# Fused attention and two feed-forward layers: scores of the next chunk placed inside the bundles of value products

## The chip, the cores and the metric

One core of a Trainium2 chip runs the whole program in one launch. The metric is device time in microseconds (us). Engines are named as in the profile: PE is TensorE (matrix products; PEld is its load of the stationary operand), DVE is VectorE, ACT is ScalarE, POOL is GpSimd, SP is SyncE, which issues all DMAs.

## What is computed

Attention for 2 batches of 8 heads, 576 positions and 64 numbers per head, with a learned bias that depends on the distance of two positions, then two feed-forward layers over the 1152 x 512 result. Cut to what matters here:

```python
def _attn_ref(q, k, v, w1, b1, w2):
    scores = scale * np.matmul(q, k.transpose(0, 1, 3, 2))
    ...
    bias = h @ w2
    scores = scores + bias.transpose(2, 0, 1)[None, :, :, :]
    scores = scores - np.max(scores, axis=-1, keepdims=True)
    attn = np.exp(scores)
    attn = attn / (np.sum(attn, axis=-1, keepdims=True) + 1e-09)
    return np.matmul(attn, v).astype(np.float32)
```

## The kernel before

The program has three stages: the bias is made (to about 64 us of the profile), attention runs (about 72 to 197 us), the two feed-forward layers follow (197 to the end).

Attention goes through eight **units**, a unit being two heads of one batch. A unit has two **jobs**, `sub` 0 with 4 chunks of 128 query rows and `sub` 1 with 5, so a unit takes nine **slots**, one chunk `n` each (`run_slot`, L464). The chunk with `n` = 2 of `sub` 1 is mixed: its rows come from both heads, and its scores take 8 products where the others take 4. Of a chunk the kernel makes:

- its **scores** (`scores`, L287): products of 288 columns into a PSUM tile `ps`, of which there are two (L154); a stationary operand of 128 x 128. PE waits here until the chunk two before has left its `ps`, and in the first chunks of a job for `ql`, the low part of q, which POOL makes (L191).
- bias and row minimum on DVE (L324, out of `ps`), the exponential on ACT (L338), sums and reciprocals on DVE (L342, L343), the scaling on POOL (L346).
- three slots (LAG) after a job's last chunk its probabilities begin to be **transposed** on PE (L373) in **pieces**, one or two pieces a slot: `PIECES` has five pieces for `sub` 0 (0, 1, 2, 3, last) and six for `sub` 1 (0, 1, 2, 3, f, last). In the next slot ACT or DVE copies the transposed piece from PSUM to `at` (L380).
- the **value products** of a whole job (`values`, L383) are done together when its last piece is there: a **bundle**. Their stationary operand is 128 x 64, so a product fills one half of the array's columns and of PSUM's partitions, the first head in one half and the second in the other. In `sub` 0 each piece has one product of 256 columns for either half. In `sub` 1 a piece has 320 columns for the first half, and 128 + 64 for the second; piece f has four products of 128 columns, all for the second half; piece last has 64 + 256 columns for either half.
- in the slot after a bundle the results are **finished** (L408): ACT copies `po` out of PSUM (L423 or L429), DVE and POOL make the splits and differences that the next layer needs.

Every engine works through its instructions in the written order (`tc.manual_schedule`, L524). Within a slot PE's order is the scores of this chunk, the transposes, and, where a job's last piece is there, the bundle. So the bundle of `sub` 0 stands between the scores of chunks 2 and 3 of the next unit's `sub` 0 (in the first unit that has one, between chunks 1 and 2), and that of `sub` 1 between chunks 3 and 4 of the next unit's `sub` 1. There are 14 such bundles while chunks are left, two in each unit but the first; the last unit's two bundles come after all chunks, in the tail (185 to 197 us).

Of the kernel before, what the change touches and what calls it, by code (L numbers as in the profile page):

```python
# [26 lines left out]
AHEAD = 2  # L27

LAG = 3

BATCHES = ((0,), (1, 2), (3,)), ((0, 1), (2, 3), (4,))

# [66 lines left out]
def tile_kernel(ctx: ExitStack, tc, qT, kT, vS, wb, wg, wv, wo, wi, wo2, table, out):  # L99
# [25 lines left out]
    with ExitStack() as actx:  # L125
# [36 lines left out]
        def load_k(i):  # L162

            pr, b = UNITS[i]
            kr = bias[0][:, :2] if i > 2 else rawp.tile([P, 2, S], F32, tag="kr", name="kr")
            load(kr, kT, pr, b)
            return dict(i=i, pr=pr, b=b, kr=kr)
# [25 lines left out]
        def prepare_k(u):  # L193


            kst = u["kst"] = kp.tile([P, 2, S], F32R, tag="kst", name="kst")
            kr = u["kr"]
            for a in range(2):
                high(kst[:, a], kr[:, a], KHIGH[a])
                yield  # L200
                for hf in range(2):
                    rows, cols = slice(D - D * hf, P - D * hf), slice(HALF * hf, HALF * (hf + 1))
                    low(kst[rows, a, cols], kst[rows, a, cols], kr[rows, a, cols], KLOW[2 * a + hf])
                yield

        def prepare_q(u, sub):


            qr = u["qr"]
            width = 704 if sub else 512  # L210
            qh = qp.tile([P, width], F32R, tag=f"qh{sub}", name="qh")
            ql = qp.tile([P, width], F32R, tag=f"ql{sub}", name="ql")
            sm = smp.tile([P, 4, 5], F32, name="sm")
            if sub == 0:
                parts = [(0, 0, 0, 256), (1, 256, 0, 256)]
                chunks = [(0, 0), (1, 0), (0, 1), (1, 1)]
            else:
                parts = [(0, 0, 256, 320), (1, 384, 256, 320)]
                nc.gpsimd.memset(qh[:, 320:384].bitcast(F32), 0.0)
                nc.gpsimd.memset(ql[:, 320:384].bitcast(F32), 0.0)  # L220
                chunks = [(0, 0), (1, 0), ("mix",), (0, 1), (1, 1)]
            u[sub] = dict(u, sub=sub, qh=qh, ql=ql, chunks=chunks, sm=sm, es=[], last=[], at={})
            for j, (a, o, s0, w) in enumerate(parts):
                high(qh[:, o : o + w], qr[:, a, s0 : s0 + w], QHIGH[2 * sub + j])
                yield
                low(ql[:, o : o + w], qh[:, o : o + w], qr[:, a, s0 : s0 + w], QLOW[2 * sub + j])
                yield
# [59 lines left out]
        def scores(u, n):  # L287

            sub, pr, kst = u["sub"], u["pr"], u["kst"]
            ch = u["chunks"][n]  # L290
            ps = psS.tile([P, 2, 512], F32, tag="S", name="ps")
            if ch[0] == "mix":
                heads = [(0, 256), (1, 320)]
                bt = bias[4][:, pr]
            else:
                a, c = ch
                heads = [(a, (448 if sub else 256) * a + P * c)]
                bt = bias[2 * sub + c][:, 2 * pr + a]

            parts = [(t, a, o) for t in ("ql", "qh") for a, o in heads]  # L300
            for hf in range(2):
                for i, (t, a, o) in enumerate(parts):
                    nc.tensor.matmul(  # L303
                        ps[:, hf, :HALF],
                        u[t][:, o : o + P],
                        kst[:, a, HALF * hf : HALF * (hf + 1)],
                        start=i == 0,
                        stop=i == len(parts) - 1,
                    )
            return ps, bt  # L310
# [72 lines left out]
        def values(u, piece):  # L383

            if piece == 0:
                u["po"] = psO.tile([P, 512], F32, name="po")
            at = u["at"].pop(piece)
            if piece == "f":
                parts = [(jc, 1, 1, 128, P * jc, 128) for jc in range(4)]
            elif piece == "last":  # L390
                mixed = [(4, 0, 0, 256, 256, D), (4, 1, 2, 256, 320, D)] if u["sub"] else []
                parts = mixed + [(4, a, a, 0, 0, 256) for a in range(2)]
            elif u["sub"]:
                parts = [(piece, 0, 0, 0, 0, 320), (piece, 1, 1, 0, 384, 128), (piece, 1, 2, 256, 320, D)]
            else:
                parts = [(piece, a, a, 0, 256 * a, 256) for a in range(2)]

            for jc, a, t, o, i, n in parts:
                v = u["v"][:, jc] if jc < 4 else u["vt"]
                nc.tensor.matmul(  # L400
                    u["po"][D * a : D * (a + 1), o : o + n],
                    v[:, D * t : D * (t + 1)],
                    at[:, i : i + n],
                    start=piece == 0 and o == 0,
                    stop=jc == 4 and o == 0,
                )
# [51 lines left out]
        chunks = [(i, sub, n) for i in range(2 * NP) for sub in range(2) for n in range(4 + sub)]  # L458
        jobs, turned, gathered, done, spare = [], [], [], [], itertools.cycle([False, True])
        prep = itertools.chain(prepare_k(units[0]), prepare_q(units[0], 0))  # L460
        before = None
        slot = 0

        def run_slot():  # L464
            nonlocal turned, done, prep, before, slot
            if slot < len(chunks):
                i, sub, n = chunks[slot]
                if n == 0:
                    for _ in prep:
                        pass  # L470
                    if sub == 0:
                        if i + 1 < 2 * NP:
                            units.append(load_k(i + 1))
                        if i == NP:
                            flat = lambda ap: ap.rearrange("p a s -> p (a s)")
                            pairs[2:] = [flat(bias[c][:, 2 * a : 2 * a + 2]) for a in range(2) for c in (2, 3)]
                            mixes[1] = flat(bias[4][:, :2])[:, : 5 * P]
                            nc.gpsimd.memset(mixes[1][:, S:], 0.0)
                        prep = prepare_q(units[i], 1)
                    elif i + 1 < 2 * NP:  # L480
                        load_qv(units[i + 1])
                        prep = itertools.chain(prepare_k(units[i + 1]), prepare_q(units[i + 1], 0))
                u = units[i][sub]
                got = scores(u, n)
            for w in done:
                w["eager"] = slot >= len(chunks) - 1
                late.append(finish(w))
                if w["eager"]:
                    next(late[-1])
            done = []  # L490
            for w, piece, got_t in turned:
                gather(w, piece, *got_t)
            if slot < len(chunks):
                biased(u, n, *got)
            if before:
                softmax(*before)
                before = None
            for _ in range(2):
                next(prep, None)
            late[:] = [steps for steps in late if next(steps, late) is not late]  # L500
            held, turned = [t[:2] for t in turned], []

            over = slot >= len(chunks)
            for _ in range(2 if slot % 9 in TWICE or over else 1):
                if jobs and jobs[0][2] <= slot:
                    w, piece, _ = jobs.pop(0)
                    turned.append([w, piece, transposes(w, piece, over and (piece == "f" or next(spare)))])
            gathered.extend(held)

            ends = [i + 1 for i, (w, piece) in enumerate(gathered) if piece == PIECES[w["sub"]][-1]]  # L510
            last_job = over and gathered and gathered[0][0] is units[-1][1]
            for _ in range(len(gathered) if last_job else max(ends, default=0)):
                w, piece = gathered.pop(0)
                values(w, piece)
                if piece == PIECES[w["sub"]][-1]:
                    done.append(w)
            if slot < len(chunks):
                before = (u, n)
                if n == 3 + sub:
                    jobs.extend((u, piece, slot + LAG) for piece in PIECES[sub])  # L520
            slot += 1
# [483 lines left out]
    with tc.manual_schedule(engines={E.PE}):  # L1005
        quads = {"z": z}
        for q in range(4):
# [5 lines left out]
            for word in f"{OTHER if q else FIRST} {TAIL}".split():  # L1013
                who, what = word
                if who in "tu":
                    n = int(what)
# [60 lines left out]
```

## Time and profile before

| | |
|---|---|
| three runs | 600.58, 601.92, 603.95 us; median 601.92 |
| profiled execution | 600.55 us, span of its instructions 598.5 us |
| PE | busy 582.8 us (97%) |
| DVE, ACT, POOL | busy 460.3, 376.2, 111.5 us |
| TensorE clock granted | 0.999 of full speed |

In the rows below a time at the start of a row is in us from the span's start. PE's products are pipelined: the durations of single rows overlap, so the text takes the distance between the starts of two rows. A product of `values` stands as two MATMUL records, one of `scores` or a transpose as one. `128*64` or `128*128` is the stationary operand. In square brackets stands the engine's idle time before a row, and who ended it.

### The profile page before, as it was taken

The numbers are of one execution on the slowest core, as the hardware profiler recorded it, in microseconds if no ns is written. First come the engines' busy times: TensorE is split into PE (matmuls) and PEld (weight loads), VectorE is DVE, ScalarE is ACT, GpSimd is POOL, SyncE is SP. The second block draws the span as 40 slices with busy tenths as digits, with TensorE's granted clock in tenths as the row PEclk, the third lists the DMA queues.
The fourth block names the chain that finished last, engine by engine and source line by source line (L and its number), as shares of the span: only waits on it lengthen the run. The fifth ranks groups of instructions, "written<-read, shape, count | busy, mean of one in ns | idle before, by whom it ended". The sixth has DMA issues, their size and how long they took to land.

```text
span 598.5 us, 11379 instructions
## 1 busy us (share of the span) xinstructions
PE 582.8 (97%) x4274; PEld 516.7 (86%) x4274; DVE 460.3 (77%) x982; ACT 376.2 (63%) x715; POOL 111.5 (19%) x165
## 2 busy tenths in 40 slices
PE   8899799999999999999999999999999999999997
PEld 6343588888887999999999999999989989988986
DVE  7999578878888999897689735679998976983432
ACT  5998787879888876665558424349835734732520
POOL 0301587878993000000000000000000000000000
PEclk9999999999999999999999999999999999999999
DMA  8979923334432333324225222122444240400012
GB/s 221 207 197 208 214 63 99 91 110 111 110 119 89 117 98 108 103 75 137 73 79 190 84 71 71 71 75 70 138 130 134 90 141 5 137 36 1 2 51 106
DMA packets 47414, 63.30 MB, mean 106 GB/s; under 512 B 4480, under 2 KB 35200, under 8 KB 47360
## 3 DMA queue, kind: packets, MB, share of 16 engines
q1 hardware_dynamic: 47360, 62.59, 36.7%
q8 instruction: 33, 0.54, 0.4%
q14 instruction: 21, 0.17, 0.1%
HBM read 49.60 MB, written 2.36 MB: 87 GB/s over the span
## 4 chain that ended last, share of the span: by engine, by line
PE 81%; DVE 7%; ACT 4%; DMA 4%; issue 2%; POOL 2%; SPq 0%; DVEq 0%; ACTq 0%; POOLq 0%
PE pw L684 37%; PE pw L992 16%; PE pw L635 13%; PE ps L303 5%; PE po L400 5%; PE pt L373 4%; DVE r L258 3%; DMA bias<-st 2%; ACT st L278 1%; DMA e<-in_qT_dram 1%; ACT r L256 1%; POOL ql L191 1%; PE pb L266 1%; ACT e L338 1%; DMA G<-in_table_dram 1%
## 5 line engine op out<-in xcount | busy, mean ns | idle before, releaser
L992 PE MATMUL pw<-oh,g2h 128*128 128x512 f32 x144 | 56.2, 390 | 0.0
L992 PE MATMUL pw<-oh,g2l 128*128 128x512 f32 x144 | 56.1, 390 | 0.0
L992 PE MATMUL pw<-ol,g2h 128*128 128x512 f32 x144 | 56.1, 389 | 0.0
L303 PE MATMUL ps<-kst,ql 128*128 128x288 f32 x160 | 49.3, 337 | 4.5 <-POOL ql L191 3.4
L266 PE MATMUL pb<-r,wb_sb 128*32 128x288 f32 x576 | 49.1, 412 | 4.4 <-ACT st L278 2.7
L258 DVE TENSOR_SCALAR r<-G 128x576 f32<-128x576 f32 x108 | 51.5, 553 | 0.1
L635 PE MATMUL pw<-gh,sh 128*128 128x384 f32 x144 | 48.4, 336 | 0.0
L635 PE MATMUL pw<-gh,sl 128*128 128x384 f32 x144 | 48.4, 336 | 0.0
L635 PE MATMUL pw<-gl,sh 128*128 128x384 f32 x144 | 48.3, 336 | 0.0
L266 PEld LDWEIGHTS pb<-r,wb_sb 128*32 128x32 f32 x576 | 20.3, 109 | 31.5 <-ACT st L278 11.5
L609 DVE SCALAR_TENSOR_TENSOR x<-raw,x 128x512 int32<-128x512 int32 x68 | 46.2, 686 | 0.9
L303 PEld LDWEIGHTS ps<-kst,ql 128*128 128x128 f32 x160 | 29.0, 188 | 16.3 <-DVE sm L324 5.7
L303 PE MATMUL ps<-kst,qh 128*128 128x288 f32 x160 | 42.6, 294 | 0.0
L324 DVE CUSTOM_DVE_ANT_0 e<-ps,bias 128x576 f32<-128x576 f32 x44 | 33.0, 749 | 9.0 <-PE ps L303 7.6
L346 POOL TENSOR_SCALAR e<-e,sm 128x576 f32<-128x576 f32 x44 | 34.1, 784 | 25.2 <-DVE sm L343 19.4
L380 ACT COPY at<-pt 128x512 f32<-128x512 f32 (+2 forms) x69 | 36.2, 547 | 3.6 <-PE pt L373 3.4
L338 ACT ACTIVATE e<-e,sm 128x576 f32<-128x576 f32 x44 | 34.3, 780 | 6.1 <-DMA vt<-in_vS_dram 3.4
L400 PE MATMUL po<-at,v 128*64 128x256 f32 (+3 forms) x384 | 36.8, 332 | 1.0 <-DVE at L380 0.8
L1030 DVE TENSOR_TENSOR acc<-pw,acc 128x512 f32<-128x512 f32 x27 | 17.5, 684 | 25.1 <-PE pw L992 25.1
L606 DVE TENSOR_SCALAR x<-x 128x512 int32<-128x512 int32 x68 | 28.7, 426 | 9.2 <-ACT x L605 5.0
L400 PEld LDWEIGHTS po<-at,v 128*64 128x64 f32 x384 | 26.6, 137 | 8.0 <-issue 1.7
L992 PEld LDWEIGHTS pw<-oh,g2l 128*128 128x128 f32 x144 | 27.0, 188 | 5.8
(272 smaller groups left out, 1678.2 us busy)
## 6 DMA issues: line engine op xcount, KB each, us to landing
raw<-in_wo_dram SPq DMA_DIRECT2D x28, 512.0 KB, 3.6
bias<-st SPq DMA_DIRECT2D x32, 288.0 KB, 4.7
raw<-in_wi_dram SPq DMA_DIRECT2D x16, 512.0 KB, 3.8
raw<-in_wv_dram SPq DMA_DIRECT2D x12, 512.0 KB, 4.2
raw<-in_wg_dram SPq DMA_DIRECT2D x12, 512.0 KB, 3.5
qr<-in_qT_dram SPq DMA_DIRECT2D x14, 288.0 KB, 4.1
v<-in_vS_dram SPq DMA_DIRECT2D x8, 384.0 KB, 3.4
bias<-in_kT_dram SPq DMA_DIRECT2D x10, 288.0 KB, 4.2
```

The lines of the kernel that those rows point to most:

```text
L258: nc.vector.tensor_scalar(r, G[:, w0 : w0 + S], PB[:, n : n + 1], 0.0, op0=ALU.add, op1=ALU.max)
L266: nc.tensor.matmul(pb[32 * ct : 32 * ct + 32, hf, :HALF], W2, rs[ct][:, HALF * hf : HALF * (hf + 1)], start=True, stop=True,)
L303: nc.tensor.matmul(ps[:, hf, :HALF], u[t][:, o : o + P], kst[:, a, HALF * hf : HALF * (hf + 1)], start=i == 0, stop=i == len(parts) - 1,)
L324: nc.vector.tensor_tensor_reduce(out=e[:, :S].rearrange("p (a n) -> p a n", a=2), in0=ps[:, :, :HALF], in1=bt.rearrange("p (a n) -> p a n" ...
L338: nc.scalar.activation(e, e, AF.Exp, bias=sm[:, 0, n : n + 1], scale=-1.0, accum_out=sm[:, 1, n : n + 1])
L346: nc.gpsimd.tensor_scalar(e, e, sm[:, 3, i : i + 1], 1.0, op0=ALU.mult, op1=ALU.mult)
L380: marks[eng, u["i"], u["sub"]] = copy(at[:, :w], pt[:, :w]).ins
L400: nc.tensor.matmul(u["po"][D * a : D * (a + 1), o : o + n], v[:, D * t : D * (t + 1)], at[:, i : i + n], start=piece == 0 and o == 0, stop ...
L609: nc.vector.scalar_tensor_tensor(yi, lw, 29, yi, op0=ALU.logical_shift_right, op1=ALU.bitwise_or)
L635: nc.tensor.matmul(ps[:, :n], w[:, k], x, start=first and k == 0 and i == 0, stop=last and k == NK - 1 and i == 2)
L684: nc.tensor.matmul(ps[:, hf, :HALF], a[:, o + k], b[:, HALF * hf : HALF * (hf + 1)], start=start and k == 0 and i == 0, stop=k == 1 and i ...
L992: nc.tensor.matmul(ps, g, w.rearrange("p k f -> p (k f)"), start=f == 0 and i == 0, stop=f == 3 and i == 2)
```

## The change

Where a bundle has given its third product group (index 2, `MIDDLE`) and the job at hand has a chunk left, the scores of that next chunk are issued at once, ahead of the fourth piece. The next slot takes them as they are and does not issue them again.

```diff
+MIDDLE = 2
...
         before = None
+        ahead = []
         slot = 0
...
                 u = units[i][sub]
-                got = scores(u, n)
+                got = ahead.pop() if ahead else scores(u, n)
...
-            for _ in range(len(gathered) if last_job else max(ends, default=0)):
+            for j in range(len(gathered) if last_job else max(ends, default=0)):
                 w, piece = gathered.pop(0)
                 values(w, piece)
+                if j == MIDDLE and slot < len(chunks) and n < 3 + sub and not ahead:
+                    ahead.append(scores(u, n + 1))
```

The order of the instructions on DVE, ACT, POOL and SP stays as it was; on PE the 14 bundles change, and nothing else. PE at a bundle of `sub` 0, third full unit, before (`po` is the value product's result, `ps` the scores, `pt` a transpose; line numbers of the kernel before):

```order
L373 MATMUL pt<-ident,m_965 128x128
L373 MATMUL pt<-ident,e_960 128x128
L400 MATMUL po<-at,v 64x256 x8
L400 MATMUL po<-at,vt_103 64x256 x2
L303 MATMUL ps<-kst,ql 128x288
L303 MATMUL ps<-kst,qh 128x288
L303 MATMUL ps<-kst,ql 128x288
L303 MATMUL ps<-kst,qh 128x288
L373 MATMUL pt<-ident,e_960 128x128
```

and the same place after the change, where two more lines at the head of the file move all line numbers on by two:

```order
L375 MATMUL pt<-ident,m_965 128x128
L375 MATMUL pt<-ident,e_960 128x128
L402 MATMUL po<-at,v 64x256 x6
L305 MATMUL ps<-kst,ql 128x288
L305 MATMUL ps<-kst,qh 128x288
L305 MATMUL ps<-kst,ql 128x288
L305 MATMUL ps<-kst,qh 128x288
L402 MATMUL po<-at,v 64x256 x2
L402 MATMUL po<-at,vt_103 64x256 x2
L375 MATMUL pt<-ident,e_960 128x128
```

The four products of scores have moved ahead of the last four value products; transposes now follow value products directly. PE at the end of a bundle of `sub` 1 in the same unit, before:

```order
L400 MATMUL po<-at,v 64x320
L400 MATMUL po<-at,v 64x128
L400 MATMUL po<-at,v 64x64
L400 MATMUL po<-at,v 64x128 x4
L400 MATMUL po<-at,vt_103 64x64 x2
L400 MATMUL po<-at,vt_103 64x256 x2
L303 MATMUL ps<-kst,ql 128x288
L303 MATMUL ps<-kst,qh 128x288
L303 MATMUL ps<-kst,ql 128x288
L303 MATMUL ps<-kst,qh 128x288
L373 MATMUL pt<-ident,e_113 128x128
```

and after:

```order
L305 MATMUL ps<-kst,ql 128x288
L305 MATMUL ps<-kst,qh 128x288
L305 MATMUL ps<-kst,ql 128x288
L305 MATMUL ps<-kst,qh 128x288
L402 MATMUL po<-at,v 64x320
L402 MATMUL po<-at,v 64x128
L402 MATMUL po<-at,v 64x64
L402 MATMUL po<-at,v 64x128 x4
L402 MATMUL po<-at,vt_103 64x64 x2
L402 MATMUL po<-at,vt_103 64x256 x2
L375 MATMUL pt<-ident,e_113 128x128
```

Here the scores have moved ahead of pieces 3, f and last: 11 of the bundle's 20 value products now come behind them.

## Rows read from the trace of the kernel before

**Rows 1.** The chain that ended last: a sub 1 bundle, and its longest piece.
```profile
116.33 3.03 PE po L400 x30
...
199.04 127.77 PE pw L684 x960
```
**Rows 2.** Windows between sub 0 bundles: length, PE busy (matmuls), PEclk, DMA share, GB/s.
```profile
74.56:91.29 16.73, 16.73 (x150) 1.00 0.32 82
91.29:107.89 16.60, 16.27 (x142) 1.00 0.42 108
107.89:123.58 15.69, 15.69 (x142) 1.00 0.35 96
123.58:140.18 16.60, 16.26 (x142) 1.00 0.37 98
140.18:156.62 16.44, 16.28 (x142) 1.00 0.41 111
156.62:173.29 16.67, 16.58 (x143) 1.00 0.26 67
```
**Rows 3.** PE's timeline at the first bundle, which follows scores without transposes between.
```profile
73.83 0.40 PE L303 MATMUL ps<-kst,ql 128*128 128x288 f32 x1
...
74.56 1.95 PE L400 MATMUL po<-at,v 128*64 128x256 f32 x16
...
76.87 0.40 PE L303 MATMUL ps<-kst,ql 128*128 128x288 f32 x1
```
**Rows 4.** PE's timeline behind another sub 0 bundle: its last products, scores, transposes.
```profile
109.67 0.60 PE L400 MATMUL po<-at,vt 128*64 128x256 f32 x4
110.20 0.40 PE L303 MATMUL ps<-kst,ql 128*128 128x288 f32 x1
...
110.84 0.38 PE L373 MATMUL pt<-ident,e 128*128 128x128 f32 x2
```
**Rows 5.** PE's timeline in the tail: the last unit's two bundles, in parts.
```profile
189.34 0.65 PE L400 MATMUL po<-at,v 128*64 128x256 f32 x4 [0.77 <-DVE at L380]
...
190.35 0.44 PE L373 MATMUL pt<-ident,e 128*128 128x128 f32 x2
190.63 0.27 PE L373 MATMUL pt<-ident,bias 128*128 128x128 f32 x1
...
192.59 1.26 PE L400 MATMUL po<-at,v 128*64 128x320 f32 x12 [0.27 <-DVE B21l L418]
193.79 0.66 PE L373 MATMUL ps<-ident,e 128*128 128x128 f32 x4
...
194.70 1.44 PE L400 MATMUL po<-at,v 128*64 128x320 f32 x17
...
196.94 0.40 PE L684 MATMUL pw<-B11h,wh 128*128 128x288 f32 x1
```
**Rows 6.** PE's timeline before a mixed chunk's scores, in two units.
```profile
113.21 0.60 PE L373 MATMUL pt<-ident,e 128*128 128x128 f32 x4
113.56 0.51 PE L303 MATMUL ps<-kst,ql 128*128 128x288 f32 x2
...
128.89 0.60 PE L373 MATMUL pt<-ident,e 128*128 128x128 f32 x4
129.69 0.54 PE L303 MATMUL ps<-kst,ql 128*128 128x288 f32 x2 [0.20 <-DVE sm L324]
```
**Rows 7.** Who waited for whom: us in total, times, longest us.
```profile
DVE e L324 <- PE ps L303: 7.6, 9, 1.4
...
DVE bias L324 <- PE ps L303: 5.1, 6, 1.1
```
**Rows 8.** Timelines of PE and DVE: a sub 1 bundle, and the mixed chunk's biased scores.
```profile
132.24 2.41 PE L400 MATMUL po<-at,v 128*64 128x320 f32 x30
...
133.65 0.74 DVE L324 CUSTOM_DVE_ANT_0 m<-ps,bias 128x576 f32<-128x576 f32 x1
```
**Rows 9.** ACT's timeline before the tail.
```profile
184.91 0.43 ACT L423 CAST B21h<-po 128x320 fp32r<-128x320 f32 x1 [1.10 <-PE po L400]
```

## What the change was expected to do

> **What bounds the kernel now.** I read the chain that ended last first. Behind attention it is PE without a break: from 199 us on one piece of 128 us after the other [rows 1]. So whatever attention wins or loses up to PE's first feed-forward product at 196.94 [rows 5] reaches the end undiminished, and the question is when PE gets there.
>
> Inside attention I cut PE's time at the starts of the `sub` 0 bundles [rows 2]. Six stretches, each a whole unit's work on PE, at the full clock in all of them. The third is 15.69 us long and PE is busy throughout: call it quiet. The second, fourth, fifth and sixth hold the same 142 or 143 matmuls and take 16.60, 16.60, 16.44 and 16.67, on average 16.58: there PE waits some 0.89 a unit. The first is 16.73, but with eight more matmuls; four transposes and the step to the next scores take 0.35 [rows 6], so eight are some 0.7 and it is nearly quiet, at 16.0. Where PE waits is seen in [rows 6]: from four transposes to the mixed chunk's scores take 0.35 in the quiet unit and 0.80 in the next one, because DVE has not yet emptied a `ps`.
>
> DVE in its turn waits for scores 15 times, 12.7 us in all [rows 7], about twice a unit, where a bundle stands in front of them. That is what the change attacks. But DVE's waiting is not PE's: in the quiet unit DVE waits as well and PE loses nothing. The whole prize is PE's waits, 4 x 0.89 and a few tenths elsewhere, about 4 us.
>
> **What the change costs on PE.** No instruction is added or removed; PE only changes more often between two kinds of work, and the bundles fall in two.
>
> A `sub` 0 bundle now: 2.31 from its start to the next scores [rows 3], and 0.64 from there to the transposes [rows 4], 2.95 together. After the change there are three steps. Second part, pieces 3 and last followed by transposes: the tail runs exactly this by itself, 189.34 to 190.35, 1.01 [rows 5]. The whole bundle has six passes more than that (each product runs twice, the halves side by side), so a pass is (2.31 - 1.01) / 6 = 0.217, and the first part, two passes more than the second, 1.44. Between them stand the scores: from scores to value products 0.73 at the one place that has this order [rows 3]. And transposes start slower behind value products, 0.28 for two [rows 5]: I add 0.06. Sum 1.44 + 0.73 + 1.01 + 0.06 = 3.24, so **+0.29**.
>
> A `sub` 1 bundle now: 3.03 [rows 1] and 0.64, together 3.67. Here the cut hurts more. A piece has 320 columns for the first half of the array and 192 for the second; pieces f and last make up for it, 832 columns against 320, so that over the bundle both halves have 1600. The second half can run ahead only while nothing else stands between. The tail shows a cut: there the same 20 products run as two pieces, 192.59 to 193.79, and the other 14 products, 194.70 to 196.94 [rows 5]: 1.20 + 2.24 = 3.44 against 3.03. The change cuts one piece later. First part: 1.20 and two passes of 320 columns, 2 x 0.217 x 320/256 = 0.54, so 1.74. Second part: its longer half has 1024 columns where the tail's 14 products have 1216, so an estimate of 2.24 x 1024/1216 = 1.89. Sum 1.74 + 0.73 + 1.89 + 0.06 = 4.42, so **+0.75**.
>
> Seven bundles of each kind: 7 x 1.04 = 7.3 us more on PE.
>
> **What it gives back.** Scores come 2.31 - 1.44 = 0.87 earlier at a `sub` 0 bundle and 3.03 - 1.74 = 1.29 at a `sub` 1 bundle, so DVE's 0.85 on average per wait goes nearly everywhere, and what it does next is ready sooner; and PE, coming later to its own waits by 0.29 or 0.75, finds them shorter for that alone. But a unit cannot be quicker than PE's own work, 15.69 + 1.04 = 16.73.
>
> By stretches: the third is quiet and pays nearly all, 0.95 (a tenth for small waits inside it); the first 0.85, with two tenths of waits to lose; so 1.8. The four long ones go from 16.58 to at least 16.73. I take 0.2 each, because one new wait appears: the scores inside a `sub` 1 bundle need the mixed chunk's `ps`. In the fourth stretch DVE works on that from 133.65 to 134.39, and the bundle starts at 132.24 [rows 8], so the third piece would be through at 132.24 + 1.74 = 133.98, and the scores stand 0.4 unless DVE is early by then. It should be by about that much, since the wait of 0.45 before the mixed chunk in that stretch is the one the `sub` 0 bundle causes. That makes 0.8, between 0 and 4 x 1.04 = 4.2.
>
> The last stretch, 173.29 to 196.94, has its own price. Before the tail ACT stands 1.10 for the result of the last bundle that is cut, with everything else of the tail queued behind [rows 9]: its exponentials, DVE's sums and copies behind them, one of which PE waits 0.77 for [rows 5]. This bundle's result comes 1.74 + 0.73 + 1.89 - 3.03 = 1.33 later, and all of that goes through; earlier scores there help nobody, since ACT's order puts the copy first. With +0.29 for the `sub` 0 bundle and 0.2 off for a wait of the usual kind: +1.4, between 0.7 (only PE's own cost less its waits) and 1.6.
>
> Together 1.8 + 0.8 + 1.4 = **+4.0 us**. The profiled execution took 600.55, so 604.55 by its rows; the median of the three runs, 601.92, is 1.37 above it, and I give the time for the median: **605.9**. The bounds: 1.6 + 0 + 0.7 = +2.3 where every wait gives way, 7.3 + 0.6 (the 1.33 in place of 0.75 at the end) = +7.9 where none does.
>
> **Rivals.**
> 1. *The waits stay.* If the long stretches are held by ACT's and POOL's queues rather than by late scores, PE's extra work adds to them: +5.5 to +7.9, some 608.5. For it: the bundle's result, which ACT and DVE finish, comes 0.87 or 1.33 later. Against: the waits lie on PE's own path, so coming later shortens them.
> 2. *The cut of `sub` 1 costs no more than that of `sub` 0.* The second part was scaled, not seen. At 0.29 for each of 14 a unit needs 15.69 + 0.58 = 16.27: the long ones gain 0.3 each, the quiet two pay 1.0 together, the end 0.5: +0.3, 602.2. Against it stands the tail's 3.44 for 3.03.
> 3. *Faster: the change of kinds is free*, weight loads being hidden. Then only waits change: the four long stretches fall to 15.69, -3.6 us, 598.3. It decides where a unit's added PE work stays under its 0.89 of waits. Against it: scores behind value products start 0.53 after the last four products' row begins, 0.31 of it after the last pass [rows 4], where a pass takes 0.217. The Trainium skill has this rival's rule on its page "TensorE: Matmul & The Clock Gate", section "Step-by-step: what each phase is for": weight loads are pulled ahead of products in flight. Its page "TensorEngine Tiling (Array Packing)", section "Key Properties", says the contrary for this case: a change of tiling mode drains the engine; by that rule, the trace agrees.
>
> That nothing moves is excluded by the order: all 14 places change.
>
> **How the numbers follow.** Forecast 0.6 (+2.3 to +5.5), first rival 0.15, second 0.19, third 0.06. About 0.5%, 3.0 us, is what a measurement here can tell from no change: the forecast lies under it in 0.07 of its 0.6. So slower 0.68, same 0.26, faster 0.06. The range goes from the second rival to the lower part of the first: 602.0 to 608.5.
>
> **What would show it.** In the profile after: `sub` 0 bundles with their scores and up to the transposes 3.2 long, `sub` 1 bundles 4.4; DVE's waits for scores well under 12.7 us; all six stretches at 16.7 to 17.0, the quiet one gone; ACT's wait before the tail 2.4 in place of 1.10. The forecast is wrong if second parts of `sub` 1 take 1.5, if the third stretch stays near 15.7, or if the long ones pass 17.3.

## The result and the profile after

| | before | after |
|---|---|---|
| median | 601.72 us (6 runs, 600.58 to 604.23) | 608.37 us (6 runs, 607.59 to 609.69) |
| profiled execution | 600.55 us, span 598.5 | 607.6 us, span 605.8 |
| PE's first feed-forward product | 196.94 [rows 5] | 204.20 |

The change makes the kernel slower by 1.1%: ratio 1.0112, 95% interval 1.0093 to 1.013, or 6.65 us between the medians. 605.9 was forecast, by a sum of +4.0. The time lies in the range, at its upper end.

In the changed kernel most line numbers are two higher than before: scores are L305, transposes L375, value products L402, DVE's biased scores L326. The chain that ended last (start, us, engine, tile, line) is shown around the sub 1 bundle of the fourth stretch, and where the feed-forward begins:

```profile
134.73 0.57 ACT kst L187
135.32 0.98 DVE kst L193
136.34 0.91 DVE T1l L420
137.24 0.60 DVE at L382
137.84 0.67 DVE m L326
138.57 0.79 PE ps L305 x4
139.36 1.91 PE po L402 x17
...
206.31 127.79 PE pw L689 x960
```

The last row answers to the second of [rows 1]: still one piece of 128 us, 7.3 later. What is new stands above it. The chain leaves PE in the middle of a bundle and goes through DVE: PE stands until DVE has read the mixed chunk's scores (tile `m`). Before, it ran through the same work of ACT and DVE in this stretch (131.13 to 133.72), but came back to PE only later, through POOL's `ql`.

The windows that answer to [rows 2], each from one sub 0 bundle's start to the next, the last one from there to the first feed-forward product (length, PE busy, PEclk, DMA share, GB/s):

```profile
74.72:93.30 18.58, 18.58 (x151) 0.94 0.25 62
93.30:110.81 17.51, 16.66 (x142) 1.00 0.36 93
110.81:127.40 16.59, 16.59 (x142) 1.00 0.38 101
127.40:144.93 17.53, 16.68 (x142) 1.00 0.34 93
144.93:162.35 17.42, 16.65 (x142) 1.00 0.35 96
162.35:179.30 16.95, 16.95 (x142) 1.00 0.32 83
179.30:204.20 24.90, 23.74 (x210) 1.00 0.34 107
```

| stretch | 1 | 2 | 3 | 4 | 5 | 6 | last |
|---|---|---|---|---|---|---|---|
| forecast change | +0.85 | +0.2 | +0.95 | +0.2 | +0.2 | +0.2 | +1.4 |
| measured change | +1.85 | +0.91 | +0.90 | +0.93 | +0.98 | +0.28 | +1.25 |

The third, the sixth and the last came as forecast. The second, fourth and fifth lost 0.9 to 1.0 each where 0.2 was expected. PE's busy time in them is 0.77 to 0.85 short of the length, so PE waits there, as it did before the change. The first stretch has a loss of its own: PEclk is 0.94.

What PE does at the two kinds of bundle, where nothing is waited for (third stretch, PE's timeline; brackets hold idle time and its releaser):

```profile
110.81 1.52 PE L402 MATMUL po<-at,v 128*64 128x256 f32 x12
112.26 0.40 PE L305 MATMUL ps<-kst,ql 128*128 128x288 f32 x1
...
112.99 0.65 PE L402 MATMUL po<-at,v 128*64 128x256 f32 x4
...
114.01 0.44 PE L375 MATMUL pt<-ident,e 128*128 128x128 f32 x2
...
119.30 1.83 PE L402 MATMUL po<-at,v 128*64 128x320 f32 x18
121.06 0.40 PE L305 MATMUL ps<-kst,ql 128*128 128x288 f32 x1
...
121.79 1.10 PE L402 MATMUL po<-at,v 128*64 128x320 f32 x11
...
123.70 0.55 PE L375 MATMUL pt<-ident,e 128*128 128x128 f32 x3
```

The sub 0 bundle is 1.45 + 0.73 + 1.02 = 3.20 long, against 2.95 before. The sub 1 bundle is 1.76 + 0.73 + 1.91 = 4.40, against 3.67. These are the forecast's 3.18 and 4.36 without its 0.06 for the transposes. In the fourth stretch the same bundle looks otherwise on PE:

```profile
135.89 1.83 PE L402 MATMUL po<-at,v 128*64 128x320 f32 x18
138.57 0.40 PE L305 MATMUL ps<-kst,ql 128*128 128x288 f32 x1 [0.85 <-DVE sm L326]
```

DVE's timeline beside it:

```profile
135.32 0.98 DVE L193 TENSOR_TENSOR kst<-bias,kst 64x288 fp32r<-64x288 f32 x1 [1.03 <-ACT kst L187]
...
137.77 0.74 DVE L326 CUSTOM_DVE_ANT_0 m<-ps,bias 128x576 f32<-128x576 f32 x1
```

From first product to scores take 2.68 in place of 1.76: PE stands 0.92, and in the second and fifth stretch 0.92 and 0.84. DVE reaches the mixed chunk 137.77 - 127.40 = 10.37 after the stretch's start. Before it was 133.65 - 123.58 = 10.07 [rows 2, 8]. So it comes 0.3 later, not earlier.

Its work did not begin late. In each unit four subtractions make the low part of `kst`, the next unit's k: three on POOL and one on DVE, which stands ahead of T1l (a low part that the next layer needs), a copy and the mixed chunk. These are DVE's and POOL's second one before the change, and POOL's second one after it:

```profile
131.73 0.46 DVE L191 TENSOR_TENSOR kst<-bias,kst 64x288 fp32r<-64x288 f32 x1 [0.79 <-ACT kst L185]
...
131.84 1.00 POOL L191 TENSOR_TENSOR kst<-bias,kst 64x288 fp32r<-64x288 f32 x1
...
135.19 0.79 POOL L193 TENSOR_TENSOR kst<-bias,kst 64x288 fp32r<-64x288 f32 x1
```

DVE's subtraction for `kst` starts 135.32 - 127.40 = 7.92 after the stretch's start, where it was 131.73 - 123.58 = 8.15: 0.23 earlier. But it takes 0.98 in place of 0.46. Before, it started ahead of POOL's second subtraction for `kst`, and POOL's took 1.00. Now POOL's three have moved forward further, from 7.38 to 6.92 after the stretch's start, so that POOL's second one starts first and takes 0.79, and DVE's is the long one. In the second stretch the same happens (0.99 in place of 0.46). In the fifth it starts 0.30 later and takes 1.59 in place of 0.46:

```profile
152.85 1.59 DVE L193 TENSOR_TENSOR kst<-bias,kst 64x288 fp32r<-64x288 f32 x1 [0.86 <-ACT kst L187]
```

In the third stretch, where DVE starts first (118.43, POOL's at 118.45), it takes 0.46 and PE does not wait.

The rows that answer to [rows 7], DVE's waits for scores (us, times, longest):

```profile
DVE e L326 <- PE ps L305: 6.2, 7, 1.7
...
DVE bias L326 <- PE ps L305: 2.6, 4, 2.0
```

And to [rows 9], ACT's timeline before the tail:

```profile
192.36 0.43 ACT L425 CAST B21h<-po 128x320 fp32r<-128x320 f32 x1 [2.48 <-PE po L402]
```

DVE waits 8.8 us for scores in place of 12.7, and ACT 2.48 in place of 1.10, as forecast.

The first stretch: PE's windows at its start.

```profile
73.50:74.72 1.22, 1.22 (x6) 0.50 1.08 227
74.72:77.20 2.48, 2.48 (x14) 0.58 0.82 182
77.20:79.00 1.80, 1.80 (x15) 1.00 0.00 0
```

PE had stood 3.10 us for POOL's `ql`, started at 72.52, and from 73.5 ran at 0.50, the lower of its two levels (1.2 GHz). The first bundle's first part took 2.45 instead of 1.45: that is the missing 1.0. The profiled execution of before waited 3.25 at the same place and kept the full clock. But it was an exception. The run `before_pool` below has no cut and the old work up to this point, and its whole first bundle takes 3.78 in place of 2.31, at a granted clock of 0.53 to 0.61. Among 70 executions of the kernel before that ran beside the experiments below, 7 have a mean clock of 0.999 or more and take 600.19 us in the median, 45 have 0.996 or 0.997 (601.86), and 18 have 0.993 or 0.994 (602.54). All six runs of after have 0.994 or 0.997. So this loss does not need the change, and the medians, which hold it on both sides, are what to compare. It is also most of why the profiled execution of before lay 1.37 under its median.

### The profile page after: what moved, and what is told of

Same layout as the page of the kernel before. It is cut to its first block, busy times and chain, and to the rows that moved or that the text cites. A ratio compares the mean times of both kernels' runs of the same rounds, so it can differ in the third digit from the quotient of the medians.

```text
span 605.8 us, 11379 instructions
## 1 busy us (share of the span) xinstructions
PE 589.9 (97%) x4274; PEld 517.2 (85%) x4274; DVE 464.3 (77%) x982; ACT 377.5 (62%) x715; POOL 111.4 (18%) x165
## 4 chain that ended last, share of the span: by engine, by line
PE 86%; DVE 5%; ACT 4%; DMA 3%; issue 2%; POOL 0%; SPq 0%; DVEq 0%; ACTq 0%; POOLq 0%
PE pw L689 37%; PE pw L997 16%; PE pw L640 12%; PE po L402 7%; PE ps L305 6%; PE pt L375 4%; DVE r L260 2%; PE pb L268 2%; DMA bias<-st 2%; ACT st L280 1%; DMA e<-in_qT_dram 1%; ACT at L382 1%; ACT e L340 1%; PE warm L532 1%; DVE kst L193 1%
## 5 line engine op out<-in xcount | busy, mean ns | idle before, releaser
L305 PE MATMUL ps<-kst,ql 128*128 128x288 f32 x160 | 49.4, 337 | 5.9 <-POOL ql L193 3.1
L268 PE MATMUL pb<-r,wb_sb 128*32 128x288 f32 x576 | 50.9, 412 | 3.3 <-DVE r L260 1.9
L402 PE MATMUL po<-at,v 128*64 128x256 f32 (+3 forms) x384 | 44.2, 341 | 1.2 <-DVE at L382 1.1
L305 PE MATMUL ps<-kst,qh 128*128 128x288 f32 x160 | 42.9, 296 | 0.0
L305 PEld LDWEIGHTS ps<-kst,ql 128*128 128x128 f32 x160 | 29.3, 190 | 15.6 <-DVE sm L326 4.9
L326 DVE CUSTOM_DVE_ANT_0 e<-ps,bias 128x576 f32<-128x576 f32 x44 | 33.0, 750 | 7.3 <-PE ps L305 6.2
L402 PEld LDWEIGHTS po<-at,v 128*64 128x64 f32 x384 | 27.2, 139 | 10.2 <-issue 4.7
```

Of the source, the lines that this page charges most:

```text
L268: nc.tensor.matmul(pb[32 * ct : 32 * ct + 32, hf, :HALF], W2, rs[ct][:, HALF * hf : HALF * (hf + 1)], start=True, stop=True,)
L305: nc.tensor.matmul(ps[:, hf, :HALF], u[t][:, o : o + P], kst[:, a, HALF * hf : HALF * (hf + 1)], start=i == 0, stop=i == len(parts) - 1,)
L326: nc.vector.tensor_tensor_reduce(out=e[:, :S].rearrange("p (a n) -> p a n", a=2), in0=ps[:, :, :HALF], in1=bt.rearrange("p (a n) -> p a n" ...
L402: nc.tensor.matmul(u["po"][D * a : D * (a + 1), o : o + n], v[:, D * t : D * (t + 1)], at[:, i : i + n], start=piece == 0 and o == 0, stop ...
```

## Experiments

**Each kind of bundle alone.** One condition more:

```diff
-                if j == MIDDLE and slot < len(chunks) and n < 3 + sub and not ahead:
+                if j == MIDDLE and not w["sub"] and slot < len(chunks) and n < 3 + sub and not ahead:
```

and `w["sub"]` for `not w["sub"]` in the second kernel.

> Only the bundles of sub 0 jobs are cut; those of sub 1 run whole, as before. Theory (the cut of sub 0 costs PE 0.29 us each, measured so after the change; nothing waits inside a sub 1 bundle, since no scores stand there): the long stretches stay within 0.2 us of before, the first and third pay 0.3 each, the last 0.3, so +0.4 us in all, 602.1; and if PE's halved clock behind its first wait comes with the cut of the first bundle, 1.0 more, 603.1. Rival (the waits of PE are not those that early scores remove): 7 x 0.29 = +2.0 without anything back, 603.7.

Measured: 603.87 us, ratio 1.0029 (1.002 to 1.0039).

> Only the bundles of sub 1 jobs are cut; those of sub 0 run whole, as before. Theory (the new wait inside the sub 1 bundle is DVE's chain in those three units, and the cut of sub 1 is what costs): PE still waits 0.9 us or more in three sub 1 bundles, the cut costs 0.73 each, and the whole is +4 to +5 us, 605.7 to 606.7; the clock stays at 0.999 if the cut of the first bundle was what halved it. Rival (the wait comes from the sub 0 cut, which lets PE reach the sub 1 bundle in another step with DVE): the three waits are under 0.3 us each and the whole is under +2.5 us, 604.2.

Measured: 607.53 us, ratio 1.0084 (1.0065 to 1.0103), above both accounts. Part of that is the start: in its profile the first bundle begins 1.46 later than in that of before and takes 4.02 in place of 2.31, at the lower clock. From the second sub 0 bundle to the first feed-forward product took 105.65 before. It is 107.26 with sub 0 alone (+1.61), 109.24 with sub 1 alone (+3.59) and 110.90 with both (+5.25): the two add up. Sub 0's 1.61 is nearer to its rival's 2.0 than to the theory's 0.4. In the second, fourth and fifth stretch nothing came back: PE now waits 0.59, 0.54 and 0.31 behind the whole sub 1 bundle. With sub 1 alone the waits inside the bundle are 0.39 and 0.45, and none in the fifth stretch. Neither account had it right: it is the same lateness of DVE, and PE meets it wherever it next needs that tile.

DVE's subtraction for `kst` in the fourth stretch, with sub 0 alone and with sub 1 alone:

```profile
133.74 0.98 DVE L193 TENSOR_TENSOR kst<-bias,kst 64x288 fp32r<-64x288 f32 x1 [1.03 <-ACT kst L187]
...
136.82 0.46 DVE L193 TENSOR_TENSOR kst<-bias,kst 64x288 fp32r<-64x288 f32 x1 [0.79 <-ACT kst L187]
```

In the second, fourth and fifth stretch it takes 1.03, 0.98 and 1.58 where sub 0 is cut, and 0.46 in all three where it is not. So the longer subtraction comes with the sub 0 cut. The waits of 0.39 and 0.45 are what the sub 1 cut makes without it. The last stretch is 23.64 with sub 0 alone and 24.92 with sub 1 alone, so its loss comes from the last sub 1 cut.

**The place of the sub 1 cut.** Behind piece f both halves of the array have had 1280 columns.

```diff
-                if j == MIDDLE and slot < len(chunks) and n < 3 + sub and not ahead:
+                if j == (4 if w["sub"] else MIDDLE) and slot < len(chunks) and n < 3 + sub and not ahead:
```

> As the change, but in a sub 1 bundle the scores stand behind piece f, the fifth, where both halves of the array have had 1280 columns. Theory (the sub 1 cut was dear because it parted the halves at 960 columns against 576, and its scores came before DVE had emptied the mixed chunk's tile): the two parts with the scores between take 0.3 us more than the whole bundle, not 0.73, no wait over 0.3 us is left inside it, and the whole is +1 us, 602.7, with 1.0 more if the clock is halved again at the start. Rival (any cut of a sub 1 bundle costs 0.7): the waits go, and the whole is +3.5 to +4.5 us, 605.2 to 606.2.

Measured: 605.48 us, ratio 1.0052 (1.0036 to 1.0069). PE's timeline in the third stretch:

```profile
119.02 2.56 PE L402 MATMUL po<-at,v 128*64 128x320 f32 x32
121.50 0.40 PE L305 MATMUL ps<-kst,ql 128*128 128x288 f32 x1
...
122.23 0.77 PE L402 MATMUL po<-at,vt 128*64 128x64 f32 x8
122.93 0.88 PE L375 MATMUL pt<-ident,e 128*128 128x128 f32 x6
```

2.48 + 0.73 + 0.70 = 3.91, against 3.67 whole and 4.40 in the change. So a cut costs 0.24 where the halves are level and 0.73 where they are 384 columns apart. The rest of the theory failed. Waits of 0.52, 0.54 and 0.31 are left inside the bundles of the second, fourth and fifth stretch, and the time is 1.8 to 2.8 above what it gave.

**What holds DVE.** In each unit DVE subtracts one quarter for the low part of `kst`, behind a wait for ACT's cast, and with the mixed chunk queued behind it. Here POOL does it.

```diff
-KHIGH, KLOW = "va", "ppvp"
+KHIGH, KLOW = "va", "pppp"
```

> As the change, but the one quarter of a unit's kst low part that DVE subtracts (0.98 us, behind a wait of up to 1.03 us for ACT) goes to POOL, which has time there. Theory (this is the work that holds DVE back from the mixed chunk in the three units with the new wait): DVE comes to the mixed chunk 1 us or more earlier, the three waits inside the sub 1 bundles fall under 0.3 us, and the time falls by 2 to 3 us against the change, to 605.4 to 606.4. Rival (DVE is held by what stands behind it, the T1 low part and ACT's copies): the waits stay over 0.6 us each and the time stays within 1 us of the change's 608.4; if POOL's third quarter comes too late for the next unit's scores, PE waits there in its place.

Measured: 605.36 us, ratio 1.0048 (1.0033 to 1.0063): 3.1 over the runs of before beside it, where the change is 6.65 over its own. The timelines of the fourth stretch's sub 1 bundle on PE and of the mixed chunk on DVE:

```profile
135.66 1.83 PE L402 MATMUL po<-at,v 128*64 128x320 f32 x18
137.42 0.40 PE L305 MATMUL ps<-kst,ql 128*128 128x288 f32 x1
...
134.92 0.75 DVE L326 CUSTOM_DVE_ANT_0 m<-ps,bias 128x576 f32<-128x576 f32 x1
```

The windows of the second to fifth stretch (length, PE busy, PEclk, DMA share, GB/s):

```profile
94.00:110.59 16.59, 16.59 (x143) 1.00 0.38 101
110.59:127.18 16.59, 16.59 (x143) 1.00 0.38 99
127.18:143.77 16.59, 16.59 (x143) 1.00 0.37 98
143.77:160.39 16.62, 16.62 (x142) 1.00 0.38 99
```

DVE reaches the mixed chunk 134.92 - 127.18 = 7.74 after the stretch's start, 2.6 earlier: T1l and a copy no longer stand behind a subtraction that waits and is long, and T1l takes 0.42 in place of 0.91. The scores follow the first part without a wait (1.76), and four stretches in a row are PE's own work and nothing else. So the new wait comes through DVE's `kst` subtraction: shown. That it is long because POOL's started first is read from the order of the rows; no run changes that order alone. And 16.59 is what the long stretches took before with their waits, 16.58: even with every wait gone, the two cuts cost what the waits had cost. At the start this kernel loses 1.3 (first bundle at 76.04, not 74.72). POOL's longer queue need not be the reason: with sub 1 alone, where POOL has the old work, the first bundle stands at 76.02. The next kernels leave the second unit's quarter with DVE all the same.

**The same quarter without the change, and with less of it.** POOL takes the quarter for units 3, 5 and 6 only, counted from 0; for every unit from 2 on in the run called all.

```diff
-                    low(kst[rows, a, cols], kst[rows, a, cols], kr[rows, a, cols], KLOW[2 * a + hf])
+                    low(kst[rows, a, cols], kst[rows, a, cols], kr[rows, a, cols], "p" if u["i"] in (3, 5, 6) else KLOW[2 * a + hf])
```

> The kernel before, without any cut, but the quarter of the kst low part that DVE subtracts goes to POOL for the fourth, sixth and seventh unit, which are prepared in the second, fourth and fifth stretch. Theory (in those stretches PE waits for DVE's own chain and not for late scores): without the change these three stretches fall from 16.6, 16.6 and 16.4 to 15.6 to 15.9 each, the others stay, and the time falls by 2 to 2.7 us, to 599.5 to 600.3. Rival (in the order before, it is the scores behind a bundle that come late, as the change supposes): the stretches stay over 16.3 and the time within 0.8 us of before's 602.3.

> The kernel before with that quarter on POOL for every unit from the third on. Theory: as with three units, and nothing for the third and fifth unit, in whose stretches DVE has no such chain; the sixth stretch (eighth unit) is open, since with all quarters on POOL it was 17.14 under the change where it had been 16.95: 599.5 to 600.5. Rival (all four long stretches have one cause): the sixth falls as well, by 0.5 or more, and the time is 0.5 us under that of the run with three units.

> The change with that quarter on POOL for the fourth, sixth and seventh unit only, so that nothing is later at the start. Theory: the three waits inside the sub 1 bundles are gone, the second to fifth stretch are all 16.6 (15.56 of PE's own work and 1.03 for two cuts), 605.5 to 606; that is 5.5 to 6 us above the kernel before with the same quarter on POOL, since now nothing of the cuts' price comes back. Rival (early scores are worth something once DVE is free): at least one of these stretches is under 16.3, or the distance to the kernel before with the same quarter is under 4.5 us.

> The sub 1 cut behind piece f, with that quarter on POOL for the three units. Theory (a sub 1 cut behind f costs PE 0.25, a sub 0 cut 0.29): the second to fifth stretch are 16.1 each, 15.56 and 0.54, and the time 603.5 to 604.2, still 3.5 to 4.5 above the kernel before with the same quarter. Rival (the wait of 0.5 inside these bundles is for something else than DVE's subtraction): it stays over 0.3 and the time stays at 605.

| | time | ratio, 95% | stretches 2 to 5 |
|---|---|---|---|
| before, quarter of 3 units | 604.02 | 1.0036 (1.0021 to 1.005) | 17.68, 15.68, 17.26, 16.80 |
| before, from the third unit on | 604.81 | 1.0047 (1.0031 to 1.0063) | 17.24, 15.72, 17.26, 17.16 |
| change, quarter of 3 units | 605.64 | 1.0062 (1.0039 to 1.0086) | 17.19, 16.59, 16.59, 16.62 |
| behind f, quarter of 3 units | 606.65 | 1.008 (1.0057 to 1.0102) | 17.20, 16.11, 17.06, 16.69 |

My theory fell here. Without the change the three stretches became longer, by 1.1, 0.7 and 0.4, and the change with the quarter on POOL is only 1.6 us above its own "before", not 5.5. Early scores are worth something once DVE is free of the quarter: they turn 17.26 into 16.59. And beside POOL's longer queue some of DVE's instructions grow. DVE in the second stretch of before with the quarter moved, one and the same cast twice:

```profile
103.00 2.29 DVE L187 CAST qh<-qr 128x256 fp32r<-128x256 f32 x1
...
105.88 0.42 DVE L187 CAST qh<-qr 128x256 fp32r<-128x256 f32 x1
```

The longest cast of `qh` was 0.59 before. Here one takes 2.29, while POOL runs four subtractions and two scalings with gaps under 0.1 (100.23 to 105.14).

**Scores ahead of the whole bundle.** No cut, so no change of kind is added.

```diff
+                if j == 0 and w["sub"] and slot < 66 and n < 3 + sub and not ahead:
+                    ahead.append(scores(u, n + 1))
                 values(w, piece)
-                if j == MIDDLE and slot < len(chunks) and n < 3 + sub and not ahead:
-                    ahead.append(scores(u, n + 1))
```

with the quarter of units 2 to 6 on POOL; the second kernel without `w["sub"]`, the third with `j == 1` in sub 0.

> The next chunk's scores stand ahead of a whole sub 1 bundle, not inside it (sub 0 bundles and the last sub 1 bundle are as before), and the DVE quarter of kst low goes to POOL for the third to seventh unit. Theory (the price of the change is the cut, and what early scores are worth is real once DVE has emptied the mixed chunk's tile): the number of changes of kind is that of before, so PE pays nothing; with the quarter on POOL the tile is empty when the bundle starts, so the scores do not wait; the second and fourth stretch fall to 15.9 to 16.2 (the wait of 0.45 before the mixed chunk stays), the fifth to 15.8, and the time to 600.0 to 601.0, 1 to 2 us under before. Rival (POOL's longer queue slows DVE so that the chain behind the bundle takes what is won): these stretches stay at 16.5 or over and the time is 602 or more.

> As the run with the scores ahead of whole sub 1 bundles, and ahead of whole sub 0 bundles too. Theory: at a sub 0 bundle DVE has not yet emptied the tile that these scores need (in the kernel before it does so 0.75 us after the bundle starts), so PE stands 0.4 to 0.8 in each of seven places, and the wait of 0.45 before the mixed chunk goes in two or three stretches: the third stretch is 16.1 to 16.4 and the time 1 to 3 us above the run with sub 1 alone. Rival (the tile is empty in time): the third stretch stays at 15.7, the long ones fall to it, and the time is 598.5 to 599.5.

> Scores ahead of whole sub 1 bundles, and in sub 0 bundles behind the first piece, where the tile should be empty. Theory (a sub 0 cut costs 0.29 wherever it stands, a sub 1 bundle left whole nothing): all stretches from the second to the fifth are 15.56 + 0.29 = 15.85 to 16.0, and the time is 600 to 601. Rival (PE still waits 0.4 or more in the second, fourth or fifth stretch): 602 or more.

Measured: 604.18 (ratio 1.003, 1.0018 to 1.0042), 612.97 (1.0188, 1.0169 to 1.0208) and 607.71 (1.0102, 1.0085 to 1.0119). The tile is not empty in time: the scores stand 0.28 to 0.55 ahead of the sub 1 bundles of the second to fifth stretch, 1.35 in the sixth, and with sub 0 included 0.8 to 1.6 at the sub 0 bundles. So with two tiles `ps` scores this early wait; a third tile was not tried. The sub 0 cut behind the first piece took 0.60 + 0.72 + 1.88 = 3.20, as behind the third: there its price does not depend on the place. But PE waited 0.6 for its scores in the second, fourth, sixth and last stretch, and 2.5 once in the sixth.

**A cheap cut only where PE waits.** Second, fourth and fifth stretch, piece f second in the sub 1 bundle, quarter of units 2 to 6 on POOL.

```diff
+            cut = slot // 9 in (2, 4, 5)
             ...
+                if cut and gathered[0][0]["sub"] and j == 1:
+                    at = [piece for _, piece in gathered].index("f")
+                w, piece = gathered.pop(at)
                 values(w, piece)
+                if cut and j == MIDDLE + w["sub"] and n < 3 + sub and not ahead:
```

> The cut only in the second, fourth and fifth stretch, where PE waited before; in their sub 1 bundles piece f stands second, so that the scores, behind four pieces, find 960 columns done in the first half of the array and 1088 in the second; the DVE quarter of kst low goes to POOL for the third to seventh unit. Theory (the dear sub 1 cut is the distance of the halves at the cut, 384 columns in the change and 128 here; PE has no other wait left): a sub 1 bundle with its scores and up to the transposes takes 4.0 to 4.1 where the change takes 4.40 and a whole bundle 3.67, the three stretches are 16.1 to 16.3, the others and the tail as before, and the time is 600.8 to 601.8, 0.5 to 1.5 us under before. Rival (the order of the pieces does not matter to the price): 4.4, three stretches of 16.6, and 602 to 603.

Measured: 604.06 us, ratio 1.0033 (1.002 to 1.0047). PE's sub 1 bundle in the second stretch, and behind it on DVE the second subtraction for T1, by the timelines:

```profile
102.39 2.12 PE L402 MATMUL po<-at,v 128*64 128x320 f32 x26
104.45 0.40 PE L305 MATMUL ps<-kst,ql 128*128 128x288 f32 x1
...
105.18 0.75 PE L402 MATMUL po<-at,v 128*64 128x320 f32 x6
...
106.41 1.09 PE L375 MATMUL pt<-ident,e 128*128 128x128 f32 x8
...
107.52 1.59 DVE L420 TENSOR_TENSOR bias<-bias,B11l 128x320 f32<-128x320 f32 x1
```

The same subtraction on DVE's timeline in the run with all quarters on POOL:

```profile
107.97 0.49 DVE L420 TENSOR_TENSOR bias<-bias,B11l 128x320 f32<-128x320 f32 x1
```

The price of the cut is as the theory says: 2.06 + 0.73 + 1.23 = 4.02, 0.35 over the whole bundle. So 0.24, 0.35 and 0.73 go with 0, 128 and 384 columns between the halves. The time is not, and lies above its rival's too: the stretches are 17.11, 17.12 and 16.92, and PE waits 0.87 before the unit's last scores in the first two. None of the twelve kernels is faster than the one before.

## Why the prediction was right, and where it failed

- **The chain** held. PE reached the feed-forward 7.26 later and the span grew by 7.3.
- **The price on PE** held, for each part: 3.20 and 4.40 for the two bundles against 3.18 and 4.36 worked out, and the scaled part at 1.91 against 1.89. The reason given for the dearer sub 1 cut, halves that can't run ahead of each other across it, fits three distances, and the sub 0 cut, where the halves are level, costs 0.25 at either of two places.
- **The first, third, sixth and last stretch** held: +0.85 without the halved clock (0.85 forecast), +0.90 (0.95), +0.28 (0.2), +1.25 (1.4). ACT's wait of 2.48 before the tail is the one that was forecast.
- **The step that failed** is the give-back in the second, fourth and fifth stretch: "the scores stand 0.4 unless DVE is early by then. It should be by about that much, since the wait of 0.45 before the mixed chunk in that stretch is the one the `sub` 0 bundle causes." That wait did go. In the second and fourth stretch DVE did start its subtraction for `kst` earlier, but by 0.23 and not by 0.4, and PE came to its bundle 0.2 earlier as well, which the sum left out. Then the subtraction took 0.99 and 0.98 in place of 0.46, and DVE was 0.3 late at the mixed chunk in place of 0.4 early. In the fifth stretch it started 0.30 later and took 1.59 in place of 0.46. The new wait was 0.92, 0.92 and 0.84, and the three stretches lost 2.8 in all where 0.6 was put. The sum took DVE's durations as they had been. The rows that could have told of the risk are in the chain that ended last: before the change it already went through ACT's cast of `kst` and DVE's T1l, copy and `m` in the second and fourth stretch, with POOL's subtractions beside them. I had read DVE's waits by their sum and not that stretch.
- **The rivals.** The first, that the waits stay, described these three stretches, and its 608.5 is next to the 608.37 measured. It named ACT's and POOL's queues; it was DVE's subtraction behind ACT's cast, grown beside POOL's. The second fell for this order (0.73, not 0.29), though 0.24 is to be had behind piece f. The third fell: no cut was free.
- **The forecast's own mark** for being wrong, long stretches past 17.3, was met. The sum of +4.0 did not come, but +6.65; the time lay in the range because that reached to the first rival, so its place there is in part luck.

What stays open: why the three long stretches stay at 17 with the quarter on POOL and cheap cuts. The stretched DVE instructions are seen in the trace, but no run took them away by themselves. A cheap sub 1 cut without the sub 0 cut and without moving the quarter was not run either, so these runs do not say whether it would pay.

## What to carry to other kernels

When work is moved forward to feed an engine that waits, first follow the instruction that would use it: what stands ahead of that instruction on its engine, and what that in turn waits for. A wait removed at one place comes back at the next one if its releaser isn't earlier, and the price of the move stays. Durations read from the trace before are not safe either: an instruction that now starts behind another engine's can take twice as long. If two streams share the array in halves, cut only where both have done the same amount.

## What the runs showed of the hardware

- PE's value products, 128 x 64, of two heads side by side: the price of putting other products between them was 0.24 to 0.25 us with both halves level, 0.35 with 128 columns between them, 0.73 with 384.
- DVE's instructions between SBUF tiles stretch while POOL runs without gaps: a cast of 0.29 to 2.29, a subtraction of 0.49 to 1.59, and in the changed kernel, beside POOL's `kst` subtractions, one of 0.46 to 0.98 and to 1.59. The Trainium skill, page "SBUF — State Buffer", section "Who interferes with whom", says that a DVE instruction with two SBUF inputs contends with a GpSimd instruction that reads SBUF, and that the later one blocks until the other is done. The subtractions have two such inputs and agree: the one that starts second is the longer, DVE's (0.98 against POOL's 0.79) or POOL's (1.00 against DVE's 0.46). The cast has one; the page allows it for casts in a two-port mode. But 2.29 is longer than any one of POOL's instructions there (0.73 to 0.86), so DVE seems to have lost to several in a row.
- PE's clock fell to its lower level behind a wait of 3.1 us in the profiled execution of after and stayed full behind 3.25 in that of before. Over 70 executions of one and the same kernel before, 63 have a mean clock below 0.999.
